# Moving the packed values to the head of the small-tile run, and four smaller moves, in a fused attention and gated feed-forward kernel

## The chip, the cores and the metric

The kernel runs on one core of a Trainium2 chip. Its time is the device time of one execution in microseconds (us): 409.43 us, the median of three runs (408.6 to 409.56). Engines are named as in the profile: PE multiplies matrices, PEld loads its weights, DVE is the vector engine, ACT the scalar engine, POOL GpSimd, SP the queue that issues DMAs.

## The reference

For each of 8 batches, 8 heads of 576 rows and 64 columns go through two attentions in a row; the result `x` (576 x 512) then goes through a gated feed-forward block:

```
p_packed = softmax(p @ k^T / 8) @ v                    # 32 packed rows a head
x        = softmax(q @ p_packed^T / 8) @ p_packed      # 576 x 64 a head
h        = relu(x @ w_in);  u, v = left and right half of h      # 512 columns each
v_n      = (v - mean(v)) / sqrt(var(v) + 1e-6)         # along the columns
v_s      = w_spatial @ v_n + b_spatial                 # along the 576 rows
out      = (u * v_s) @ w_out
```

All of it is float32, and the kernel keeps that precision by splitting numbers in a high and a low part (`_h`, `_l`) and multiplying high by high, high by low and low by high.

## The kernel before

The program works batch by batch, and the loop over `b` (line 1108) is a pipeline three batches deep, written by hand: while the feed-forward block of batch `b` runs (`ff`, `att`), the query attention of `b + 1` (`nxt`) is prepared, the packed values of `b + 2` (`far`) are made, and the packed scores of `b + 3` (`further`). PE, DVE, ACT and POOL keep the order in which the calls stand (lines 35 to 46), so each engine is a strict queue; the SP queue issues loads and stores in order too.

PSUM is cut into four tiles of two banks, `q0` to `q3`, handed round by name: a new user of a tile waits until the last reader of the old content is done. SBUF tiles come from pools under a tag; tag `o` (two buffers) holds the kept half of the last value chunk (`part`) and the four output blocks of a batch; tag `vn` (two buffers) holds the split of `T3` and `T4`; tags `v_h` and `v_l` (one buffer each) hold the split values and, later in the batch, the product parts `P1`, `P5`, `P57` and `U`.

One batch on PE has these stages: `value` (the right half of `x @ w_in`, three groups of row chunks, each summed over the two halves `r` of the heads); turns of small matrices; `up` (the left half); then a run of small matmuls, in order `query_scores` (names `qT,ppT`), `mix(1)` (`w_in_sb,ppT`: the packed rows times one half of `w_in`, so that the query weights can be applied to that product), `pack_values` (`v_sb,p1T`), `mix(0)`, `pack_scores` (`kT,pT`); then the four `gate` groups (`wsp_h,v_h` and so on); then seven `product` blocks of 12 matmuls, by which the 2 x 2 blocks of the last matrix product are made from seven products: A11, S1, A12 (summed onto A11), S4 (onto S1), S3, S2, A22 (onto S3).

Beside the gates and products, DVE and ACT make the query softmax of `nxt` in halves 0 and 1 (`query_max`, `query_sub`, `query_exp`, `query_sum`, `query_norm`, `query_turn`, `query_hi`, `query_lo`, `query_tail`), apply the gate (`gated`), and form and split the blocks (`block_sum`, `block_hi`, `block_lo`: `g21`, `g22`, `T1` to `T4`). A product that is summed onto a PSUM tile waits until that tile has been read (`keep_part` for P1 and P5, `add_part` for P57). At the end come `U = P1 + S2`, `out12 = U + S4`, `out22 = U + P57`, `out21 = U + A22`, each written to its own tile of tag `o` and stored.

Of the kernel before, what the change touches and what calls it, by code (L numbers as in the profile page):

```python
# [11 lines left out]
F32 = mybir.dt.float32  # L12
F32R = mybir.dt.float32r
AF = mybir.ActivationFunctionType
ALU = mybir.AluOpType
# [4 lines left out]
P = 128  # L20
B, H, S, D, NP = 8, 8, 576, 64, 32
DM, DF = 512, 1024
FH = DF // 2
# [26 lines left out]
def body(ctx: ExitStack, tc, q, k, v, vt, p, w_in, w_sp, b_sp, w_out, out):  # L50
# [11 lines left out]
    pe, dve, act, pool = (  # L62
        InOrder(tc, e) if x in PIN else e
        for e, x in ((nc.tensor, "t"), (nc.vector, "v"), (nc.scalar, "s"), (nc.gpsimd, "g"))
    )
# [4 lines left out]
    two = ctx.enter_context(tc.tile_pool(name="two", bufs=2))  # L70
    small = ctx.enter_context(tc.tile_pool(name="small", bufs=3))
    psum = ctx.enter_context(tc.tile_pool(name="ps", bufs=1, space=bass.MemoryType.PSUM))

    def on(i):

        return lambda: psum.tile([P, 2, 512], F32, tag=f"ps{i}", name=f"ps{i}_t")

    def by_turns(*quarters):
        turn = itertools.cycle([on(i) for i in quarters])
        return lambda: next(turn)()  # L80
# [4 lines left out]
    def mm(out_ap, lhsT, rhs, start, stop, more=False):  # L85

        pe.matmul(out_ap, lhsT=lhsT, rhs=rhs, start=start, stop=stop, skip_group_check=more)
# [27 lines left out]
    def load_v(b):  # L115
        v_sb = io.tile([P, NC + 1, H * D], F32, tag="v", name="v_sb")
        nc.sync.dma_start(v_sb[:, :NC, :], v[b])
        nc.sync.dma_start(v_sb[:TAIL, NC, :], vt[b])
        loaded["v", b] = v_sb
# [111 lines left out]
    A11, A12, A22, S1, S2, S3, S4, A21 = range(8)  # L231
# [70 lines left out]
    class Attention:  # L302
# [172 lines left out]
        def mix(self, x, psum):  # L475
# [4 lines left out]
            for r in range(2):  # L480
                for j in range(NJ):
# [5 lines left out]
                        True,  # L487
                    )

        def mix_hi(self, x, rs=slice(0, 2)):  # L490
            act.copy(self.m_h[:, x, rs, :], self.ms[x][:, rs, :])

# [4 lines left out]
    class FeedForward:  # L497
# [12 lines left out]
        def chunks(self, g):  # L510
            return [c for c in (2 * g, 2 * g + 1) if c <= NC]

        def value(self, g, psum=None, js=(0, 1), ns=(0, 1, 2)):
            a_h, a_l, m_h, m_l = (getattr(self.att, x) for x in ("a_h", "a_l", "m_h", "m_l"))
            if g not in self.ps:
                self.ps[g] = psum()
            terms = ((a_h, m_h), (a_h, m_l), (a_l, m_h))
            if g == 2:
                terms = terms[:2]
            steps = [(r, n) for r in range(2) for n in range(len(terms))]  # L520
            if self.b == 0:
                steps.sort(key=lambda rn: rn[1])
            for r, n in steps:
                if n not in ns:
                    continue
                aa, ww = terms[n]
                for i in js[: len(self.chunks(g))]:
                    c = 2 * g + i
                    mm(
                        self.ps[g][:, i, :],  # L530
                        aa[:, r, c * P : (c + 1) * P],
                        ww[:, 1, r, :],
                        (r, n) == steps[0],
                        (r, n) == steps[-1],
                    )
# [241 lines left out]
            self.put(o, 0, 1)  # L777

        def out21(self, fs=slice(0, 2)):
            if fs.start == 0:  # L780
                self.o21 = self.out_block()
            self.add_part(self.o21, "U", A22, fs)
            self.put(self.o21, 1, 0, fs)

        def out22(self):
            o = self.out_block()
            dve.tensor_tensor(o, self.part("U"), self.part("P57"), op=ALU.add)
            self.put(o, 1, 1)


# [16 lines left out]
    att, nxt, far, further = (Attention(b) for b in range(4))  # L807
    keep_warm(2, 9)
    att.pack_scores(by_turns(0, 3))
    ff = FeedForward(0, att)  # L810
# [296 lines left out]
    q0, q1, q2, q3 = 1, 2, 3, 0  # L1107
    for b in range(1, B):
        att, nxt, far = nxt, far, further
        further = Attention(b + 3) if b + 3 < B else None  # L1110
        ff = FeedForward(b, att)
        ff.value(2, psum=on(q0))
        ff.value(0, psum=on(q1))
        ff.relu(2)
        ff.value(1, psum=on(q2))
        ff.relu(0)
        ff.relu_tail()
        ff.stats(2)
        ff.inverse(2)
        ff.stats(0)  # L1120
        ff.inverse(0)
        ff.relu(1)
        if far:
            far.pack_turn(on(q3), ff.ps[2])
        if nxt:
            nxt.packed_turn(ff.ps[2])
            nxt.packed_turned()
        if far:
            far.pack_turned()
        ff.stats(1)  # L1130
        ff.inverse(1)
        ff.norm(2)
        ff.norm(0)
        ff.up(0, psum=on(q1))
        ff.up_relu(0)
        ff.norm_hi(0)
        ff.norm(1)
        ff.norm_lo(0)
        ff.up(1, psum=on(q2))
        ff.norm_hi(2)  # L1140
        ff.up_relu(1)
        ff.up(2, psum=on(q0))
        ff.up_relu(2)
        ff.tail_hi()
        ff.norm_lo(2)
        ff.up(3, psum=on(q3))
        ff.up_relu(3)
        ff.norm_hi(1)
        if nxt:
            nxt.query_scores(psum=by_turns(q1, q2))  # L1150
            nxt.query_tiles()
            if far:
                load_q(b + 2)
            nxt.mix(1, psum=on(q0))
            nxt.query_spread(0)
            nxt.query_spread(1)
            nxt.mix_hi(1)
            if far:
                far.pack_values(on(q3))
                far.packed()  # L1160
                if further:
                    load_v(b + 3)
            nxt.mix_lo(1)
        ff.norm_lo(1)
        if nxt:
            nxt.mix(0, psum=on(q1))
            nxt.mix_hi(0)
            if further:
                further.pack_scores(psum=by_turns(q2, q3))
                if b + 4 < B:  # L1170
                    load_k(b + 4)
                for r in range(2):
                    further.pack_max(r)
                    further.pack_exp(r)
            nxt.mix_lo(0)
            nxt.query_max(0)
            nxt.query_sub(0)
            nxt.query_exp(0)
            if further:
                further.pack_sum()  # L1180
        if further:
            turns = (q0, q1, q2, q3)
        else:
            turns = (q3, q2, q0, q1) if nxt else (q1, q2, q0, q3)
        if not nxt:
            for cs in ((0, 1), (2, 3)):
                ff.gate((0, 1), "hm", cs, psum=by_turns(*turns[:2]))
        for e, i in enumerate(turns):
            ff.gate((e,), "hmlt" if nxt or e > 1 else "lt", psum=on(i))
            if nxt and e == 1:  # L1190
                nxt.query_sum(0)
                nxt.query_norm(0)
            ff.gated(e)
            if nxt and e == 0:
                nxt.query_max(1)
                nxt.query_sub(1)
                nxt.query_exp(1)
            elif e == 1:
                ff.block_hi("g11")
                ff.block_sum("T1")  # L1200
                ff.block_hi("T1")
                ff.block_lo("g11")
                if nxt:
                    nxt.query_turn(0)
                    nxt.query_hi(0)
                ff.block_lo("T1")
            elif nxt and e == 2:
                nxt.query_lo(0)
                nxt.query_tail(0)
                nxt.query_sum(1)  # L1210
                nxt.query_norm(1)
        ff.product(A11, "g11", psum=on(turns[0]))
        ff.block_hi("g21")
        ff.block_sum("T3")
        ff.block_lo("g21")
        ff.keep_part("P1", A11)
        ff.block_hi("g22")
        ff.block_sum("T2")
        ff.product(S1, "T1", psum=on(turns[1]))
        ff.block_hi("T3")  # L1220
        ff.block_lo("g22")
        ff.keep_part("P5", S1)
        ff.block_lo("T3")
        ff.block_hi("T2")
        ff.product(A12, "g21", onto=A11)
        ff.out11()
        ff.block_sum("T4")
        ff.block_lo("T2")
        ff.block_hi("T4")
        ff.product(S4, "g22", onto=S1)  # L1230
        ff.block_lo("T4")
        if nxt:
            nxt.query_turn(1)
            nxt.query_hi(1)
        ff.product(S3, "T3", psum=on(turns[2]))
        ff.add_part("P57", "P5", S3)
        if nxt:
            nxt.query_lo(1)
            nxt.query_tail(1)
        ff.product(S2, "T2", psum=on(turns[3]))  # L1240
        ff.add_part("U", "P1", S2)
        ff.out12()
        ff.product(A22, "T4", onto=S3)
        if nxt:
            ff.out22()
            ff.out21()
        else:
            for f in range(2):
                ff.out21(slice(f, f + 1))
            ff.out22()  # L1250
        q0, q1, q2, q3 = turns[0], turns[1], turns[3], turns[2]


_INS = ["q", "k", "v", "vt", "p", "w_in", "w_sp", "b_sp", "w_out"]
# [51 lines left out]
```

## Time and profile before

| | us |
|---|---|
| median of the runs | 409.43 (408.6 to 409.56) |
| the profiled execution: its own time | 407.98 |
| the profiled execution: its span, first to last instruction | 406.2 |
| busy: PE, DVE, ACT, POOL | 394.9, 332.9, 192.7, 74.1 |

The profile is of one execution, and all rows below are of it. PE's matmuls overlap at their ends, so the time from one matmul's start to the next one's start is what a matmul costs; the "us" of a group runs from its first start to its last modelled end. A timeline merges equal instructions that follow each other. All helpers record through line 43, so groups are told apart by the names of their tiles.

### The profile page before, as it was taken

To read this page: it belongs to the slowest core of one execution; us is meant where nothing else is said; L and a number is where in the kernel's file an instruction comes from. 1 tells how busy PE (TensorE), PEld (TensorE's weight loads), DVE (VectorE), ACT (ScalarE), POOL (GpSimd) and SP (SyncE) were. 2 spreads that over 40 slices of the span, in tenths; PEclk is the share of its full clock that TensorE was granted. 3 is DMA by queue.
4 is the path that set the end of the run, shared out by engine and by line. 5 is a ranking of instruction groups with operands and counts; after the bars stand their busy time and mean duration, and the time that the engine had idled before them with its cause. 6 is when DMAs were issued, how large, how long until landed. Compare 5 with 4: busy or idle time off the path is not lost.

```text
span 406.2 us, 8936 instructions
## 1 busy us (share of the span) xinstructions
PE 394.9 (97%) x3800; PEld 354.5 (87%) x3800; DVE 332.9 (82%) x567; ACT 192.7 (47%) x291; POOL 74.1 (18%) x98
## 2 busy tenths in 40 slices
PE   7999999999999999999999999999999999999993
PEld 5768977799799879999699888999799889999993
DVE  2597799979799779977899788995899789978563
ACT  3587865766435353434634273244634272526140
POOL 1566445644000120002100030001200030004000
PEclk9999999999999999999999999999999999999998
DMA  7999057730810227020530205002300200020002
GB/s 306 382 383 397 20 178 305 241 116 2 293 66 31 87 81 278 2 85 34 224 129 31 87 13 225 0 29 89 120 0 30 87 2 2 0 102 17 2 30 88
DMA packets 16620, 46.62 MB, mean 115 GB/s; under 512 B 1346, under 2 KB 10562, under 8 KB 13764
## 3 DMA queue, kind: packets, MB, share of 16 engines
q1 hardware_dynamic: 16580, 46.05, 31.1%
q8 instruction: 30, 0.49, 0.5%
q14 instruction: 10, 0.08, 0.1%
HBM read 36.61 MB, written 9.44 MB: 113 GB/s over the span
## 4 chain that ended last, share of the span: by engine, by line
PE 94%; DVE 3%; POOL 1%; issue 1%; DMA 1%; POOLq 0%; DVEq 0%
PE ps_t L43 94%; DVE nmax L43 1%; POOL bits L43 1%; DMA out_t<-o 1%; DVE bits L43 0%; DVE t L43 0%; DVE o L43 0%; DVE sm_t L43 0%; DVE w_in_sb L43 0%; DVE pp L43 0%; DVE mx L43 0%; DVE prod L43 0%; POOL ident masks.py:199 0%; DVE rtot L43 0%; POOL ident masks.py:197 0%
## 5 line engine op out<-in xcount | busy, mean ns | idle before, releaser
L43 PE MATMUL ps_t<-wsp_h,v_h 128*128 128x288 f32 x256 | 55.9, 300 | 0.0
L43 PE MATMUL ps_t<-wsp_l,v_h 128*128 128x288 f32 x256 | 54.5, 295 | 0.0
L43 POOL TENSOR_TENSOR rstd<-mv,eps 128x2 f32<-128x2 f32 (+2 forms) x26 | 6.9, 265 | 245.5 <-DVE mv L43 245.4
L43 PE MATMUL ps_t<-t,wout_h 128*128 128x288 f32 x232 | 48.3, 294 | 0.0
L43 PEld LDWEIGHTS ps_t<-wsp_h,v_h 128*128 128x128 f32 x256 | 40.8, 188 | 3.8 <-DVE m_l L43 1.9
L43 PEld LDWEIGHTS ps_t<-wsp_l,v_h 128*128 128x128 f32 x256 | 41.5, 189 | 0.0
L43 ACT CAST g_h<-u 128x576 fp32r<-128x576 f32 x24 | 16.1, 674 | 49.4 <-DVE u L43 49.1
L43 PE MATMUL ps_t<-wsp_h,v_l 128*128 128x288 f32 x256 | 39.4, 296 | 0.0
L43 PEld LDWEIGHTS ps_t<-t,wout_h 128*128 128x128 f32 x232 | 38.0, 188 | 0.0
L43 PEld LDWEIGHTS ps_t<-wsp_h,v_l 128*128 128x128 f32 x256 | 35.9, 189 | 0.5 <-issue 0.5
L43 PE MATMUL ps_t<-t,wout_l 128*128 128x288 f32 x116 | 32.3, 294 | 0.0
L43 PE MATMUL ps_t<-g_h,wout_h 128*128 128x288 f32 x104 | 30.1, 305 | 0.6 <-DVE pp L43 0.6
L43 PE MATMUL ps_t<-g_h,wout_l 128*128 128x288 f32 x104 | 29.1, 295 | 0.0
L43 PE MATMUL ps_t<-a_h,m_h 128*128 128x288 f32 x128 | 28.1, 301 | 0.0
L43 PE MATMUL ps_t<-a_h,m_l 128*128 128x288 f32 x128 | 27.4, 296 | 0.0
L43 PE MATMUL ps_t<-a_l,m_h 128*128 128x288 f32 x128 | 27.4, 296 | 0.0
L43 DVE TENSOR_TENSOR u<-ps_t,u 128x576 f32<-128x576 f32 x28 | 21.0, 749 | 7.3 <-PE ps_t L43 7.3
L43 PE MATMUL ps_t<-m_l,a_h 128*128 128x512 f32 x80 | 25.8, 390 | 0.0
L43 PE MATMUL ps_t<-m_h,a_h 128*128 128x512 f32 x80 | 25.8, 391 | 0.0
L43 ACT ACTIVATE sm_t<-sm_t 128x576 f32<-128x576 f32 x16 | 11.0, 685 | 27.5 <-DVE sm_t L43 23.7
L43 DVE TENSOR_TENSOR o<-ps_t,prod 128x576 f32<-128x576 f32 (+1 forms) x15 | 10.7, 717 | 15.4 <-DMA out_t<-o 15.1
L43 ACT COPY part<-ps_t 64x512 f32<-64x512 f32 x8 | 4.7, 583 | 39.2 <-DVE o L43 39.2
(136 smaller groups left out, 989.6 us busy)
## 6 DMA issues: line engine op xcount, KB each, us to landing
out_t<-o SPq DMA_DIRECT2D x31, 288.0 KB, 2.3
v_sb<-in_v SPq DMA_DIRECT2D x8, 1024.0 KB, 8.1
qT<-in_q SPq DMA_DIRECT2D x7, 1152.0 KB, 5.4
kT<-in_k SPq DMA_DIRECT2D x7, 1152.0 KB, 8.4
raw<-in_w_in SPq DMA_DIRECT2D x4, 1024.0 KB, 12.7
raw<-in_w_out SPq DMA_DIRECT2D x2, 1024.0 KB, 9.8
kT<-in_k SPq DMA_DIRECT2D x2, 576.0 KB
qT<-in_q SPq DMA_DIRECT2D x2, 576.0 KB, 12.8
```

The costliest lines, as they stand in the source:

```text
L43: return lambda *a, **k: self.tc.keep_in_program_order(call(*a, **k))
```

## The change

`pack_values` and `packed` move from between the two mixes to the head of the small-tile run. Both mixes follow each other, and each is copied whole out of PSUM by ACT (`mix_keep`, into tag `vn`); its high part is then cast from that copy, its low part formed from it. The PSUM tiles are handed out in another order. `query_sum(1)` and `query_norm(1)` move from the third gate into the products, the splits of the blocks are reordered, and the value groups 2 and 0 are made by halves of the heads, so that half 1 of the query weights is needed later. `out21` and `out22` are formed in place, in `U` and in `P57`; in the last batch `out22` comes ahead of `out21`.

```diff
+        def mix_keep(self, x):
+            kept = two.tile([P, 2, FH], F32, tag="vn", name="kept")
+            act.copy(kept, self.ms[x])
+            self.ms[x] = kept
...
-        def value(self, g, psum=None, js=(0, 1), ns=(0, 1, 2)):
+        def value(self, g, psum=None, js=(0, 1), ns=(0, 1, 2), rs=(0, 1)):
...
-                if n not in ns:
+                if n not in ns or r not in rs:
...
-            if fs.start == 0:
-                self.o21 = self.out_block()
-            self.add_part(self.o21, "U", A22, fs)
-            self.put(self.o21, 1, 0, fs)
+            o = self.part("U")
+            self.add_part(o, "U", A22, fs)
+            self.put(o, 1, 0, fs)
...
-            o = self.out_block()
-            dve.tensor_tensor(o, self.part("U"), self.part("P57"), op=ALU.add)
+            o = self.part("P57")
+            dve.tensor_tensor(o, self.part("U"), o, op=ALU.add)
...
-        ff.value(2, psum=on(q0))
-        ff.value(0, psum=on(q1))
+        for r in range(2):
+            ff.value(2, psum=on(q0), rs=(r,))
+            ff.value(0, psum=on(q1), rs=(r,))
...
+        if far:
+            far.pack_values(on(q1))
+            far.packed()
+            if further:
+                load_v(b + 3)
         if nxt:
-            nxt.query_scores(psum=by_turns(q1, q2))
+            s0, s1, m1, m0 = (q2, q0, q3, q1) if far else (q1, q2, q0, q3)
+            nxt.query_scores(psum=by_turns(s0, s1))
             nxt.query_tiles()
             if far:
                 load_q(b + 2)
-            nxt.mix(1, psum=on(q0))
             nxt.query_spread(0)
+            nxt.mix(1, psum=on(m1))
+            nxt.mix_keep(1)
             nxt.query_spread(1)
+            nxt.mix(0, psum=on(m0))
+            nxt.mix_keep(0)
             nxt.mix_hi(1)
...
-            turns = (q0, q1, q2, q3)
+            turns = (q3, q1, q2, q0)
         else:
-            turns = (q3, q2, q0, q1) if nxt else (q1, q2, q0, q3)
+            turns = (q2, q0, q3, q1) if far else (q1, q2, q0, q3)
...
-                nxt.query_sum(1)
-                nxt.query_norm(1)
...
+        if nxt:
+            nxt.query_sum(1)
+        ff.keep_part("P5", S1)
...
+            ff.out22()
             for f in range(2):
                 ff.out21(slice(f, f + 1))
-            ff.out22()
-        q0, q1, q2, q3 = turns[0], turns[1], turns[3], turns[2]
+        q0, q1, q2, q3 = turns[0], turns[3], turns[1], turns[2]
```

On PE, the end of `up` and the small-tile run of a batch with all four stages (`v_sb` the packed values, `qT` the query scores, `w_in_sb` the mixes, `kT` the packed scores, `wsp_h` the first gate). Before:

```order
L43 MATMUL ps_t<-a_h,m_l 128x288 x2
L43 MATMUL ps_t<-qT,ppT 32x288 x16
L43 MATMUL ps_t<-w_in_sb,ppT 32x512 x8
L43 MATMUL ps_t<-v_sb,p1T 32x64 x40
L43 MATMUL ps_t<-w_in_sb,ppT 32x512 x8
L43 MATMUL ps_t<-kT,pT 32x288 x16
```

The same place on PE in the change:

```order
L43 MATMUL ps_t<-a_h,m_l 128x288 x2
L43 MATMUL ps_t<-v_sb,p1T 32x64 x40
L43 MATMUL ps_t<-qT,ppT 32x288 x16
L43 MATMUL ps_t<-w_in_sb,ppT 32x512 x16
L43 MATMUL ps_t<-kT,pT 32x288 x16
L43 MATMUL ps_t<-wsp_h,v_h 128x288 x2
```

The packed values stand ahead of the query scores, and the two mixes are one piece of 16.

On DVE, from the fourth `gated` (`u<-ps_t,u`) to the end of the products of the same batch (`sm` the query sum, `at` the query turn, `prod<-ps_t,prod` first P57 and then U). Before, with the two rows of the query sum that lead up to it:

```order
L43 RECIPROCAL sm<-sm 128x18
L43 TENSOR_TENSOR sm_t<-sm_t,sm 128x576
L43 TENSOR_TENSOR u<-ps_t,u 128x576
L43 TENSOR_TENSOR u<-u 128x2x288
...
L43 TENSOR_TENSOR t<-u,t 128x576
L43 TENSOR_TENSOR g<-u,g 128x576
L43 TENSOR_TENSOR t<-g,t 128x576 x2
L43 STREAM_TRANSPOSE at<-sm_t 128x576
L43 TENSOR_TENSOR prod<-ps_t,prod 128x576
L43 TENSOR_TENSOR a_l<-at,a_h 128x576
L43 CAST a_h<-a_l 128x64
L43 TENSOR_TENSOR prod<-ps_t,prod 128x576
```

The same place on DVE in the change:

```order
L43 TENSOR_TENSOR t<-u,t 128x576
L43 TENSOR_REDUCE sm<-sm_t 128x18
L43 TENSOR_SCALAR sm<-sm 128x18
L43 RECIPROCAL sm<-sm 128x18
L43 TENSOR_TENSOR t<-g,t 128x576
L43 TENSOR_TENSOR sm_t<-sm_t,sm 128x576
L43 TENSOR_TENSOR g<-u,g 128x576
L43 STREAM_TRANSPOSE at<-sm_t 128x576
L43 TENSOR_TENSOR prod<-ps_t,prod 128x576
L43 TENSOR_TENSOR t<-g,t 128x576
L43 TENSOR_TENSOR a_l<-at,a_h 128x576
L43 CAST a_h<-a_l 128x64
```

The sum and the norm of half 1 stand behind the fourth `gated` and ahead of P57; the low part of T4 (the last `t<-g,t`) stands behind P57.

On DVE, the end of the last batch. Before:

```order
L43 TENSOR_TENSOR t<-g,t 128x576 x2
L43 TENSOR_TENSOR prod<-ps_t,prod 128x576 x2
L43 TENSOR_TENSOR o<-ps_t,prod 128x576
L43 TENSOR_TENSOR o<-ps_t,prod 128x288 x2
L43 TENSOR_TENSOR o<-prod 128x576
```

In the change:

```order
L43 TENSOR_TENSOR t<-g,t 128x576
L43 TENSOR_TENSOR prod<-ps_t,prod 128x576
L43 TENSOR_TENSOR o<-ps_t,prod 128x576
L43 TENSOR_TENSOR prod<-prod 128x576
L43 TENSOR_TENSOR prod<-ps_t,prod 128x288 x2
```

`out22` stands ahead of the two halves of `out21`, and both are written into the product parts instead of a tile of tag `o`.

## Rows read from the trace of the kernel before

**Rows 1.** The page: PE's busy time, and the chain that ended last.

```profile
PE 394.9 (97%) x3800; PEld 354.5 (87%) x3800; DVE 332.9 (82%) x567; ACT 192.7 (47%) x291; POOL 74.1 (18%) x98
...
PE 94%; DVE 3%; POOL 1%; issue 1%; DMA 1%; POOLq 0%; DVEq 0%
```

**Rows 2.** PE timeline of batch 2's small-tile run: start us, us, what.

```profile
147.12 0.42 PE L43 MATMUL ps_t<-a_h,m_l 128*128 128x288 f32 x2
147.47 1.23 PE L43 MATMUL ps_t<-qT,ppT 64*32 64x288 f32 x32
148.46 1.27 PE L43 MATMUL ps_t<-w_in_sb,ppT 64*32 64x512 f32 x16
149.66 1.68 PE L43 MATMUL ps_t<-v_sb,p1T 128*32 128x64 f32 x76
151.13 0.63 PE L43 MATMUL ps_t<-w_in_sb,ppT 64*32 64x512 f32 x4
...
152.07 1.38 PE L43 MATMUL ps_t<-kT,pT 64*32 64x288 f32 x32
```

**Rows 3.** PE timeline of batch 6's run, which has no packed values.

```profile
332.45 2.18 PE L43 MATMUL ps_t<-w_in_sb,ppT 64*32 64x512 f32 x32
334.56 0.53 PE L43 MATMUL ps_t<-wsp_h,v_h 128*128 128x288 f32 x2
```

**Rows 4.** PE timeline of batch 3's run.

```profile
193.81 1.83 PE L43 MATMUL ps_t<-qT,ppT 64*32 64x288 f32 x28
...
196.67 1.68 PE L43 MATMUL ps_t<-v_sb,p1T 128*32 128x64 f32 x76
```

**Rows 5.** PE timeline of batch 5's run.

```profile
287.12 1.72 PE L43 MATMUL ps_t<-qT,ppT 64*32 64x288 f32 x28
...
289.88 1.68 PE L43 MATMUL ps_t<-v_sb,p1T 128*32 128x64 f32 x76
```

**Rows 6.** DVE timeline, 184 to 279: the last output block of batches 2 and 4.

```profile
184.71 0.76 DVE L43 TENSOR_TENSOR o<-ps_t,prod 128x576 f32<-128x576 f32 x1 [4.10 <-DMA out_t<-o]
...
277.92 0.76 DVE L43 TENSOR_TENSOR o<-ps_t,prod 128x576 f32<-128x576 f32 x1 [4.00 <-DMA out_t<-o]
```

**Rows 7.** DVE timeline of the end of the last batch.

```profile
399.09 1.61 DVE L43 TENSOR_TENSOR o<-ps_t,prod 128x576 f32<-128x576 f32 x3
402.23 0.76 DVE L43 TENSOR_TENSOR o<-prod 128x576 f32<-128x576 f32 x1 [1.53 <-DMA out_t<-o]
```

**Rows 8.** PE timeline of batch 1's products, around the start of A12.

```profile
124.98 0.43 PE L43 MATMUL ps_t<-t,wout_h 128*128 128x288 f32 x2
125.32 0.40 PE L43 MATMUL ps_t<-g_h,wout_h 128*128 128x288 f32 x1
125.56 0.30 PE L43 MATMUL ps_t<-g_h,wout_l 128*128 128x288 f32 x1
```

**Rows 9.** ACT timeline of the same stretch: the cast of g21, the copy of P1.

```profile
124.06 0.67 ACT L43 CAST g_h<-u 128x576 fp32r<-128x576 f32 x1 [4.10 <-DVE u L43]
124.64 0.63 ACT L43 COPY prod<-ps_t 128x576 f32<-128x576 f32 x1
```

**Rows 10.** DVE timeline of batch 1, 121 to 132: query sum, fourth gated, P57, low part.

```profile
121.31 0.75 DVE L43 TENSOR_REDUCE sm<-sm_t 128x18 f32<-128x576 f32 x1
...
123.28 0.75 DVE L43 TENSOR_TENSOR u<-ps_t,u 128x576 f32<-128x576 f32 x1
...
130.48 0.76 DVE L43 TENSOR_TENSOR prod<-ps_t,prod 128x576 f32<-128x576 f32 x1
131.15 0.75 DVE L43 TENSOR_TENSOR a_l<-at,a_h 128x576 fp32r<-128x576 f32 x1
```

**Rows 11.** PE timeline of batch 1: first product's start, and the value group behind the last.

```profile
122.08 0.29 PE L43 MATMUL ps_t<-g_h,wout_h 128*128 128x288 f32 x1
...
133.43 0.39 PE L43 MATMUL ps_t<-m_h,a_h 128*128 128x512 f32 x1
```

**Rows 12.** ACT timeline of batch 1's run: a pass over a whole mix.

```profile
103.44 1.01 ACT L43 CAST m_h<-ps_t 128x1024 fp32r<-128x1024 f32 x1 [0.61 <-PE ps_t L43]
```

More of the change, by code (lines that the diff above doesn't have):

```diff
@@ L1153, in body @@
                 load_q(b + 2)
-            nxt.mix(1, psum=on(q0))
             nxt.query_spread(0)
+            nxt.mix(1, psum=on(m1))
+            nxt.mix_keep(1)
             nxt.query_spread(1)
+            nxt.mix(0, psum=on(m0))
+            nxt.mix_keep(0)
             nxt.mix_hi(1)
[L1158 to L1163, printed above, removed]
         ff.norm_lo(1)
         if nxt:
-            nxt.mix(0, psum=on(q1))
-            nxt.mix_hi(0)
             if further:
-                further.pack_scores(psum=by_turns(q2, q3))
+                further.pack_scores(psum=by_turns(s0, s1))
                 if b + 4 < B:
@@ L1174, in body @@
                     further.pack_exp(r)
-            nxt.mix_lo(0)
+            nxt.mix_lo(1)
+            nxt.mix_hi(0)
             nxt.query_max(0)
@@ L1178, in body @@
             nxt.query_exp(0)
+            nxt.mix_lo(0)
             if further:
@@ L1214, in body @@
         ff.block_sum("T3")
+        ff.block_hi("T3")
         ff.block_lo("g21")
         ff.keep_part("P1", A11)
+        ff.block_sum("T2")
         ff.block_hi("g22")
-        ff.block_sum("T2")
         ff.product(S1, "T1", psum=on(turns[1]))
-        ff.block_hi("T3")
         ff.block_lo("g22")
-        ff.keep_part("P5", S1)
         ff.block_lo("T3")
         ff.block_hi("T2")
+        if nxt:
+            nxt.query_sum(1)
+        ff.keep_part("P5", S1)
         ff.product(A12, "g21", onto=A11)
         ff.out11()
+        ff.block_lo("T2")
+        if nxt:
+            nxt.query_norm(1)
         ff.block_sum("T4")
-        ff.block_lo("T2")
         ff.block_hi("T4")
         ff.product(S4, "g22", onto=S1)
-        ff.block_lo("T4")
         if nxt:
@@ L1236, in body @@
         ff.add_part("P57", "P5", S3)
+        ff.block_lo("T4")
         if nxt:
```

## The prediction, made before the change was timed

> **What bounds the kernel now.** First the page: PE is busy 394.9 of a span of 406.2 us, and 94% of the chain that ended last is PE's [rows 1]. So PE is idle for some 11 us, in the first batch, which the change leaves as it is, and at the end of the program. Nothing can be won by making DVE or ACT faster as such; a gain must come from a matmul that starts sooner after the one before it, or from that end. I therefore read PE's timeline by starts, and looked for places where the next start is later than that of equal matmuls elsewhere (0.13 us apart for 288 columns, 0.23 for 512). There are four kinds.
>
> First, the run of small tiles. The query scores, in tiles of 64x32, start at 147.47; the mix follows 0.99 later, the packed values, in tiles of 128x32, 1.20 later, the second mix 1.47 later, and the packed scores, again in 64x32, 0.94 after that [rows 2]. The same mix costs 1.20 where the tile shape changes behind it and 0.94 where it stays. Batch 6 has no packed values, and its two mixes with a change of shape behind take 334.56 - 332.45 = 2.11 [rows 3]: 0.91 for the first if the second takes 1.20.
>
> Second, late landings. In batches 3 and 5 the scores and first mix take 196.67 - 193.81 = 2.86 and 289.88 - 287.12 = 2.76 [rows 4, 5], against 149.66 - 147.47 = 2.19 in batch 2 [rows 2]. The cause stands a stage earlier on DVE: the last output block of the batch before waits 4.10 and 4.00 us for a store that has to leave its buffer of tag `o` [rows 6]. Behind that block, in the queues of DVE and ACT, stand `part`, the statistics and the splits of the next batch, up to the relus that free the PSUM tiles for the query scores.
>
> Third, the end. DVE does U, out12 and out21 from 399.09 on, then out22 idles for the same kind of landing and starts at 402.23 [rows 7].
>
> Fourth, the products. A12's first matmul is due at 125.24 (two starts behind 124.98), starts at 125.32, and the next comes 0.24 later instead of 0.13 [rows 8]: 0.08 of wait and 0.10 of restart. It waited for the copy of P1, which ran 124.64 to 125.27 behind the cast of g21 on ACT [rows 9], and that cast waited for the fourth `gated`, held on DVE by the query sum and norm of half 1, 121.31 to 123.28 [rows 10]. S4 shows the 0.10 again. Batches 1, 2, 3, 4 and 6 have this, some 0.28 each.
>
> **The change part by part.** The order of the small tiles: with the packed values ahead of the scores, the first mix has the second behind it, in its own shape, and takes 0.91 instead of 1.20. The change of shape from `up` to the first small tile stands as before, the packed values end in tiles of 64x32 and have the scores behind them where they had the second mix. So 0.29 a batch goes, in the five batches (1 to 5) that have the stage: **1.43 us**. No row shows `up` followed by the packed values. The nearest is `up` followed by the scores, two starts at 0.13 and then 0.35 from the first to 147.47, so 0.09 lost [rows 2]; I take that, which changes nothing. Bounds: a change of shape costs at least that 0.09 of drain and at most the 0.29, so the term lies between 0.45 and 1.43. The Trainium skill says that a change of tiling mode, not of tile, drains TensorE (TensorEngine Tiling (Array Packing), Key Properties). By the rule alone every switch is only such a drain, and at 0.09 each the sum would be 1.0 us smaller; the row prices this one at 0.29, because half of the tiles run behind the others when the mix ends.
>
> The mixes copied whole: two copies and two casts of ACT a batch where two casts were; a pass is 1.01 us [rows 12], so 2.0 us of ACT are added beside the gates, where ACT is idle for whole microseconds (4.10 before one cast [rows 9]). They free the PSUM tiles of gates 0 and 1 sooner than the low parts did. Priced at nothing. If the cover fails, the first gate waits for a copy that ends about 1 us behind its mix, while the second mix and the packed scores (0.94 + 1.31) run.
>
> The output blocks in place: no block waits for a landing any more, so the two late runs fall back to 2.19: 0.67 + 0.57 = **1.24 us**. The other batches lose DVE's ordinary wait there too (1.53 in the last one [rows 7]), which cost PE nothing.
>
> The end: out22 comes before out21 and has no landing to wait for. DVE's queue is U, out12 at 399.09, out22, then the halves of out21, which wait for no landing and whose product was done in time for them before: without out22 they and out12 end at 399.09 + 1.61 = 400.70, and with one more block at 0.67 [rows 10] at 401.4. Before, the last block ends at 402.23 + 0.76 = 402.99. The last store goes **1.55 us** earlier; it is issued behind three others, and half as big. Bounds: 1.2 if the stores queue, 1.7 if the smaller one lands sooner.
>
> The products: here the change adds waits. Behind the fourth `gated` DVE now has the splits, the query sum and norm, T4, the turn and only then P57, for which A22 waits. I add it up from the start of that `gated`, about 0.22 behind A11's: 0.78 to the cast of g21 (123.28 to 124.06 [rows 9, 10]) and as much again until T3 is formed, 0.58 and 0.55 on ACT for the cast of T3 and the copy of P1, 0.70 for the cast of g22 [rows 9]: 3.4 when its low part starts on DVE. From there five blocks, the turn counted as one, at 0.67 (130.48 to 131.15 [rows 10]), and the sum and norm, 1.97 [rows 10]: P57 starts at 8.7 and ends at 9.4, that is 9.6 behind A11. Seven products take 133.43 - 122.08 = 11.35 [rows 11] less 0.28 of waits, 1.58 each; A22 is due 9.48 behind A11. It waits some 0.15, and 0.10 for the restart. Next on DVE come the low part of T4 (0.67), the low query weights (0.78), their tail (0.1, taken) and U (0.76), ending 11.9 behind A11. The value group 0 now takes the tile that U reads (it took that of out12), and is due at 9.48 + 0.25 + 1.58 + 0.45 = 11.76: 0.15 more. The wait for P1 goes: its copy now ends 0.22 + 0.78 + 0.78 + 0.58 + 0.63 = 3.0 behind A11, and A12 is due at 3.16. S4's restart stays, 0.10. Old waits 0.28, new ones 0.4 to 0.45: **0.15 us** lost in each of five batches, and 0.4 in batch 5, which had none: 1.15 us. Bounds: no wait at all, a gain of 1.4, to waits of 0.8 a batch, a loss of 3.4. The value order by halves is priced at nothing: the same 28 matmuls; it moves the need for half 1 back by six matmuls, and DVE is that much later with it.
>
> **Sum**: -1.43 - 1.24 - 1.55 + 1.15 = -3.1 us. The profiled execution's time is 407.98, which gives 404.9. The median shown is 409.43, 1.45 above it; no row says why. If more late landings make up that excess, at 0.6 each, the change takes them too; if not, it gives 406.3. I forecast 405.9.
>
> **Rivals.** The products lose nothing: DVE and ACT run 0.3 sooner than added up, the waits for P57 and U vanish and the old ones too. For it: the new waits are differences of 0.15 between sums of ten durations. Against it: U ends that chain with no gap in DVE's queue. 405.9 - 1.15 - 1.4 = 403.4.
>
> The change of shape costs only a drain, and moves to another border: 1.0 less is won, 406.9. For it: 0.09 behind `up` [rows 2]. Against it: 0.91 beside 1.20 [rows 3].
>
> DVE becomes the bound: the chain from the fourth `gated` to U is 0.3 longer a batch than added up, because ACT's casts stand between its links. Six batches: 407.7. For it: every link waits for another engine.
>
> Slower than before: the same chain, with its end at value group 0, which cannot start before U has read its tile. Each 0.1 us of the chain costs 0.1 in six batches. It decides from 0.7 a batch on, when the low mix parts, now behind the packed maxima, hold the third and fourth `gated` so that the gate's end no longer starts the chain; with 0.9 a batch 5.4 us are lost against 3.1 won beside the forecast's waits: 411.3. Against it: DVE gets back its idle time before the last block (1.53 to 4.10 [rows 6, 7]), and what moves behind the gate is 1.97.
>
> The change does little beyond its end: the late landings do not occur in the timed runs and the drain is cheap, 408.5.
>
> **Chances.** The forecast 0.55 (its own range 404.4 to 407.2), no loss in the products 0.14, cheap drain 0.11, DVE the bound 0.11, little beyond the end 0.05, slower 0.04. A measurement of this kernel can tell about 0.3%, 1.2 us, from no change: faster means under 408.2, slower over 410.7. Of DVE the bound a fifth lies above 408.2, so faster 0.55 + 0.14 + 0.11 + 0.09 = 0.89, rounded to 0.88; same 0.08; slower 0.04. The range 403.4 to 408.2 leaves out 1 to 2 in 10.
>
> **What the profile after would show.** Right: two mixes as one piece of 1.85 with the packed scores behind, the small-tile run 0.29 shorter, batches 3 and 5 with no longer runs than the others; no DVE wait for a landing of an output block; the last DVE block at an end near 401.4; small waits of A22 for P57 and of a value group for U. Wrong: a piece of the run that takes longer by what the mix lost, a first gate that waits for a copy, or waits in the products over 0.6 a batch.

## The result, and the profile after

The change makes the kernel faster: 404.88 us, the median of 4 runs (404.78 to 405.54), against 409.34 of before in the same comparison (4 runs, 408.6 to 409.56). The ratio is 0.9898, with a 95% interval of 0.9881 to 0.9915. The forecast was 405.9 with a range of 403.4 to 408.2. The profiled execution took 404.85, its span is 403.1: 3.1 less than before.

The page of the kernel after, PE's busy time and the chain that ended last, beside [rows 1]:

```profile
PE 392.6 (97%) x3800; PEld 356.9 (89%) x3800; DVE 332.2 (82%) x567; ACT 204.4 (51%) x303; POOL 74.1 (18%) x98
...
PE 93%; DVE 3%; DMA 1%; ACT 1%; issue 1%; POOL 1%; SPq 0%; DVEq 0%; POOLq 0%; ACTq 0%
```

PE still sets the time. ACT's 11.7 us more are the copies of the mixes, and nothing waits for them. For the rest I add up PE's timeline by stages, from one stage's first start to the next one's, over batches 1 to 7 (small tiles: 1 to 6); "end" runs from the last matmul's start to the end of the span (406.21 and 403.06 to two places). The differences are taken before rounding.

| us | small tiles | gates | products | value | end |
|---|---|---|---|---|---|
| before | 32.68 | 105.08 | 78.79 | 44.64 | 6.66 |
| after | 29.82 | 105.09 | 79.51 | 44.99 | 5.23 |
| difference | -2.87 | +0.02 | +0.72 | +0.36 | -1.44 |

Turns and `up` are equal to 0.01. The sum is -3.2, and the first batch ended 0.08 later, which gives the 3.1 of the span. So the gain is in the small tiles and at the end, and a quarter of it is paid back in the products and the value groups.

First the start of the first gate in batches 2 and 3 of the kernel before, where the runs of [rows 2, 4] end; then PE's timeline of the kernel after, the small-tile runs of batches 2, 3 and 5 (start us, us, what):

```profile
153.38 0.53 PE L43 MATMUL ps_t<-wsp_h,v_h 128*128 128x288 f32 x2
...
200.39 0.53 PE L43 MATMUL ps_t<-wsp_h,v_h 128*128 128x288 f32 x2
```

```profile
147.24 1.73 PE L43 MATMUL ps_t<-v_sb,p1T 128*32 128x64 f32 x80
148.79 1.20 PE L43 MATMUL ps_t<-qT,ppT 64*32 64x288 f32 x32
149.76 2.13 PE L43 MATMUL ps_t<-w_in_sb,ppT 64*32 64x512 f32 x32
151.48 1.38 PE L43 MATMUL ps_t<-kT,pT 64*32 64x288 f32 x32
152.79 0.53 PE L43 MATMUL ps_t<-wsp_h,v_h 128*128 128x288 f32 x2
...
193.36 1.73 PE L43 MATMUL ps_t<-v_sb,p1T 128*32 128x64 f32 x80
...
198.90 0.53 PE L43 MATMUL ps_t<-wsp_h,v_h 128*128 128x288 f32 x2
...
288.06 2.13 PE L43 MATMUL ps_t<-w_in_sb,ppT 64*32 64x512 f32 x32
290.11 0.53 PE L43 MATMUL ps_t<-wsp_h,v_h 128*128 128x288 f32 x2
```

Read it by starts. From the packed values to the first gate it is 152.79 - 147.24 = 5.55 in batch 2 and 198.90 - 193.36 = 5.54 in batch 3; before it was 153.38 - 147.47 = 5.91 and, in batch 3, 200.39 - 193.81 = 6.58. Both mixes take 151.48 - 149.76 = 1.72 with the packed scores behind them, in their own shape; in batch 5, which has no packed scores, the same 32 matmuls take 290.11 - 288.06 = 2.05 with the gate's full tiles behind. Add start and us of a group and compare with the next start: where the shape changes, the next group starts only 0.07 to 0.08 before the group ahead ends (290.11 against 288.06 + 2.13; before, 149.66 against 148.46 + 1.27), where it stays, 0.41 before (151.48 against 149.76 + 2.13). So the price of a change is what the last matmuls ahead have still to run. (The ends are modelled, the starts are not.)

DVE's U of the last batch in the kernel before; then DVE's timeline of the kernel after at the end of batch 2 and of the last batch, beside [rows 6, 7]; then the SP queue's last issues:

```profile
398.30 0.76 DVE L43 TENSOR_TENSOR prod<-ps_t,prod 128x576 f32<-128x576 f32 x1 [0.82 <-PE ps_t L43]
```

```profile
180.28 0.75 DVE L43 TENSOR_TENSOR prod<-prod 128x576 f32<-128x576 f32 x1
181.13 0.76 DVE L43 TENSOR_TENSOR prod<-ps_t,prod 128x576 f32<-128x576 f32 x1
...
396.59 0.76 DVE L43 TENSOR_TENSOR prod<-ps_t,prod 128x576 f32<-128x576 f32 x1
...
398.06 0.75 DVE L43 TENSOR_TENSOR prod<-prod 128x576 f32<-128x576 f32 x1
398.91 0.82 DVE L43 TENSOR_TENSOR prod<-ps_t,prod 128x288 f32<-128x288 f32 x2
```

```profile
398.83 1.42 SPq L770 DMA_DIRECT2D out_t<-prod  x3
```

No output block has an idle time in brackets any more. From the start of U to the end of the last block it is 398.91 + 0.82 - 396.59 = 3.14 us; before it was 402.99 - 398.30 = 4.69.

The products of batch 1 in the kernel after: PE at A11, around A12 and S4 and in A22, then DVE's fourth `gated`, P57, the low part of T4 and U, beside [rows 8, 10, 11]:

```profile
121.73 0.29 PE L43 MATMUL ps_t<-g_h,wout_h 128*128 128x288 f32 x1
...
124.63 0.43 PE L43 MATMUL ps_t<-t,wout_h 128*128 128x288 f32 x2
124.90 0.34 PE L43 MATMUL ps_t<-g_h,wout_h 128*128 128x288 f32 x1
125.07 0.29 PE L43 MATMUL ps_t<-g_h,wout_l 128*128 128x288 f32 x1
...
126.55 0.38 PE L43 MATMUL ps_t<-g_h,wout_h 128*128 128x288 f32 x1
126.75 0.30 PE L43 MATMUL ps_t<-g_h,wout_l 128*128 128x288 f32 x1
...
132.00 0.64 PE L43 MATMUL ps_t<-t,wout_h 128*128 128x288 f32 x3
132.47 0.29 PE L43 MATMUL ps_t<-t,wout_l 128*128 128x288 f32 x1
```

```profile
121.93 0.76 DVE L43 TENSOR_TENSOR u<-ps_t,u 128x576 f32<-128x576 f32 x1 [0.39 <-PE ps_t L43]
...
130.54 0.72 DVE L43 TENSOR_TENSOR prod<-ps_t,prod 128x576 f32<-128x576 f32 x1
131.18 0.73 DVE L43 TENSOR_TENSOR t<-g,t 128x576 fp32r<-128x576 f32 x1
...
132.73 0.75 DVE L43 TENSOR_TENSOR prod<-ps_t,prod 128x576 f32<-128x576 f32 x1
```

A12 starts on time (124.90, two starts behind 124.63), and loses 0.04 to its restart; S4 loses 0.07; in A22 three matmuls take 0.47 instead of 0.40. The first of these three, at 132.00, is A22's fifth matmul, the first to use the low part of T4, which ends on DVE at 131.18 + 0.73 = 131.91; the change put it behind P57. This costs 0.06 to 0.08 in each of batches 1 to 6. In batches 3 to 6 A22's first matmul is late too, by 0.10 to 0.13 with its restart: the wait for P57. In batches 1 and 2 it is not; there the 34 starts between S4 and A22 take 4.57 instead of 4.48, a few nanoseconds each, and no row says why. The fourth `gated` now starts 0.20 behind A11 instead of 1.20, and DVE waits for PE there. P57 starts 130.54 - 121.73 = 8.81 behind A11.

### The profile page after: what moved, and what is told of

Read it like the earlier page. It is cut to its first block, busy times and chain, and to the rows that moved or that the text cites. A ratio compares the mean times of both kernels' runs of the same rounds, so it can differ in the third digit from the quotient of the medians.

```text
span 403.1 us, 8924 instructions
## 1 busy us (share of the span) xinstructions
PE 392.6 (97%) x3800; PEld 356.9 (89%) x3800; DVE 332.2 (82%) x567; ACT 204.4 (51%) x303; POOL 74.1 (18%) x98
## 4 chain that ended last, share of the span: by engine, by line
PE 93%; DVE 3%; DMA 1%; ACT 1%; issue 1%; POOL 1%; SPq 0%; DVEq 0%; POOLq 0%; ACTq 0%
PE ps_t L43 93%; DMA kT<-in_k 1%; DVE nmax L43 1%; POOL bits L43 1%; DVE prod L43 0%; ACT p L43 0%; DVE t L43 0%; DVE sm_t L43 0%; DVE w_in_sb L43 0%; ACT raw L43 0%; DVE pp L43 0%; DVE mx L43 0%; DVE o L43 0%; SPq L112 0%; SPq L108 0%
## 5 line engine op out<-in xcount | busy, mean ns | idle before, releaser
L43 PE MATMUL ps_t<-t,wout_h 128*128 128x288 f32 x232 | 49.4, 298 | 0.0
L43 ACT ACTIVATE vr<-ps_t 128x1024 f32<-128x1024 f32 (+1 forms) x18 | 16.7, 932 | 19.0 <-PE ps_t L43 19.0
L43 DVE BATCH_NORM_STATS2 bn<-vr 128x6 f32<-128x512 f32 x32 | 20.4, 673 | 3.8 <-ACT vr L43 3.7
```

The lines of the kernel that those rows point to most:

```text
L43: return lambda *a, **k: self.tc.keep_in_program_order(call(*a, **k))
```

## Experiments

Each kernel was compared with the kernel before on its own chip, so medians of different comparisons stand up to 0.8 us apart by their before (409.34 to 408.54). The stages are of the one profiled run.

| kernel | us, median (runs) | ratio to before, 95% | small tiles | products | value |
|---|---|---|---|---|---|
| before | 409.34 (4) | | 32.68 | 78.79 | 44.64 |
| after | 404.88 (4) | 0.9898 [0.9881, 0.9915] | 29.82 | 79.51 | 44.99 |
| before, blocks in place in all but the last batch | 407.18 (10) | 0.9968 [0.9948, 0.9987] | 31.46 | 78.84 | 44.63 |
| before, blocks in place, `out22` earlier | 405.6 (5) | 0.9932 [0.9905, 0.9958] | 31.46 | 78.73 | 44.63 |
| after, packed values between the mixes | 406.46 (8) | 0.9941 [0.9925, 0.9956] | 31.41 | 79.49 | 44.97 |
| after, scores ahead of the packed values | 405.91 (1) | | 30.62 | 79.44 | 44.95 |
| after, sum and norm at the third gate | 412.91 (4) | 1.0104 [1.0074, 1.0134] | 29.81 | 87.90 | 44.63 |
| after, value groups whole | 404.56 (4) | 0.9896 [0.9868, 0.9924] | 29.81 | 79.49 | 44.66 |
| after, query turn behind P57 | 403.5 (4) | 0.9877 [0.9857, 0.9896] | 29.81 | 78.66 | 44.74 |
| the same, copies of P1 and P5 ahead of casts | 402.27 (4) | 0.9848 [0.9827, 0.9869] | 29.82 | 77.33 | 44.61 |
| the same, query sum in the gap for ACT | 402.43 (4) | 0.9848 [0.9827, 0.9869] | 29.82 | 77.33 | 44.56 |
| after, low mix parts formed from PSUM | 421.06 (1) | | 41.76 | 79.24 | 45.00 |

**The output blocks alone.** The kernel before, with the two blocks formed in place in all batches but the last:

```diff
         def out21(self, fs=slice(0, 2)):
+            if self.b < B - 1:
+                o = self.part("U")
+                self.add_part(o, "U", A22, fs)
+                self.put(o, 1, 0, fs)
+                return
...
-            o = self.out_block()
+            o = self.part("P57") if self.b < B - 1 else self.out_block()
```

> The kernel before with one part of the change alone: out21 and out22 formed in place in batches 1 to 6, the last batch and all else as before. In the trace the stage that gives here is the small-tile run of batches 3 and 5 (2.86 and 2.76 us up to the packed values instead of 2.19). Theory L: the blocks' wait for a slow landing costs PE about 0.6 us each time, the profiled execution of before had two, and the 1.4 us by which the median of before (409.34) stands above its profiled execution (407.98) are more of them: the median here comes to 406.6 to 407.0, and every run lies close to it. Rival: the excess of the median is something else: 409.34 - 1.24 = 408.1. Both: no DVE wait for a landing in batches 1 to 6, small-tile runs of batches 3 and 5 as long as the others (5.91, and 4.7 in batch 5, which has no packed scores), end as before (6.7 us from PE's last start to the end of the span).

It took 407.18 (just above the 406.6 to 407.0 expected), 1.9 under its own before (409.05 over 17 runs, 406.99 to 409.96). PE's run of batch 3 in this kernel:

```profile
194.05 1.23 PE L43 MATMUL ps_t<-qT,ppT 64*32 64x288 f32 x32
195.04 1.27 PE L43 MATMUL ps_t<-w_in_sb,ppT 64*32 64x512 f32 x16
196.24 1.68 PE L43 MATMUL ps_t<-v_sb,p1T 128*32 128x64 f32 x76
```

The 2.86 of [rows 4] are 2.19 here, and batch 5 loses its 0.56 too: from 32.68 to 31.46, 1.23 before rounding, the forecast term, by this edit alone. The median moves by 0.6 more than that, and the spread goes: nine of these ten runs lie within 0.5 us, the 17 of before over 3.0. So the edit takes away most of the excess of the median of before over its profile. That it was late landings, of which the timed runs had more than the profiled one, is inferred; the timed runs leave no trace.

**With the end as well**: the two blocks in place in all batches, and `out22` ahead of `out21` in the last.

```diff
...
-            self.add_part(self.o21, "U", A22, fs)
-            self.put(self.o21, 1, 0, fs)
+            o = self.part("U")
+            self.add_part(o, "U", A22, fs)
+            self.put(o, 1, 0, fs)
...
-            o = self.out_block()
+            o = self.part("P57")
...
+            ff.out22()
             for f in range(2):
                 ff.out21(slice(f, f + 1))
-            ff.out22()
```

> Kernel before with the output blocks alone changed: out21 and out22 in place in all batches, and out22 ahead of out21 in the last one. Theory: the end gives its 1.40 on top of what the blocks in place give, whatever stands ahead of it: 406.99 - 1.40 = 405.6, ratio to before some 0.991, with small-tile runs as in the in-place run (5.91, and 4.71 in batch 5). Rival: part of the end's 1.40 came from the products of the last batch, which the other edits moved, and the end alone gives under 1.0: 406.0 or more.

405.6, and an end of 403.4 - 398.20 = 5.2 us from the last matmul: the edit gives the 1.4 by itself, and the rival falls. DVE's last blocks in this kernel stand as in the kernel after, with the same 0.85 between `out22` and `out21`:

```profile
398.42 0.75 DVE L43 TENSOR_TENSOR prod<-prod 128x576 f32<-128x576 f32 x1
399.27 0.82 DVE L43 TENSOR_TENSOR prod<-ps_t,prod 128x288 f32<-128x288 f32 x2
```

**The order of the small tiles.** The kernel after with the packed values back between the mixes, and with the PSUM tiles as before:

```diff
-            far.pack_values(on(q1))
-            far.packed()
...
             nxt.mix_keep(1)
+            if far:
+                far.pack_values(on(q3))
+                far.packed()
...
```

> The change with the packed values back between the two mixes, and the PSUM tiles of that run as before; the whole copies, the products and the outputs stay as in the change. Theory S: the mix pays for the change of tile shape behind it, so the run is 5.9 us again in batches 1 to 4 against 5.55, 4.7 in batch 5 against 4.58, and the median is 404.88 + 4 x 0.36 + 0.13 = 406.4. Rival: the gain came from the other PSUM tiles and the copies, by which nothing waits; the run stays at 5.55 to 5.65 and the median at 404.9 to 405.3.

406.46, and the runs are 5.91 again:

```profile
148.96 1.27 PE L43 MATMUL ps_t<-w_in_sb,ppT 64*32 64x512 f32 x16
150.16 1.68 PE L43 MATMUL ps_t<-v_sb,p1T 128*32 128x64 f32 x76
151.63 0.63 PE L43 MATMUL ps_t<-w_in_sb,ppT 64*32 64x512 f32 x4
...
152.57 1.38 PE L43 MATMUL ps_t<-kT,pT 64*32 64x288 f32 x32
```

The mixes take 1.20 + 0.94, each as before the change, with the copies still there: the order makes the 0.36, not the copies. The PSUM tiles went back together with the order, but none of these rows has an idle time in brackets, and the next kernel moves the values with the tiles of the change kept.

**Which small tiles pay.** The kernel after with the scores first, then the packed values, then both mixes:

```diff
-            far.pack_values(on(q1))
-            far.packed()
...
             nxt.query_scores(psum=by_turns(s0, s1))
             nxt.query_tiles()
...
+            far.pack_values(on(q1))
+            far.packed()
             nxt.query_spread(0)
             nxt.mix(1, psum=on(m1))
```

> Kernel after with the query scores ahead of the packed values, both mixes still one piece behind them. It tells where the price of leaving the 128x32 and 64x32 tiles lies. Theory S (any of the small kinds pays some 0.36 once, when the packed values' tile shape follows it in the middle): the run is as long as with the values between the mixes, 5.91, and the scores take some 1.3 instead of 0.97; time about 406.4. Rival (only the wide 512-column mixes pay it, since half of their tiles trail at the end): the run stays at 5.55 and the time at 404.9.

Neither: the run is 5.76.

```profile
147.82 1.23 PE L43 MATMUL ps_t<-qT,ppT 64*32 64x288 f32 x32
148.98 1.68 PE L43 MATMUL ps_t<-v_sb,p1T 128*32 128x64 f32 x76
...
152.24 1.40 PE L43 MATMUL ps_t<-kT,pT 64*32 64x288 f32 x32
153.58 0.53 PE L43 MATMUL ps_t<-wsp_h,v_h 128*128 128x288 f32 x2
```

The scores take 1.16 instead of 0.97, so a shape change behind 288 columns costs 0.19, less than behind 512 (0.34 with the same packed values behind: 1.20 against half of 1.72), and it is paid once. The packed values again start 0.07 before the scores end (148.98 against 147.82 + 1.23). Of the three places tried, the packed values stand best where full tiles, not small ones, are ahead of them.

**The sum and norm back at the third gate**, the rest of the change kept:

```diff
                 nxt.query_tail(0)
+                nxt.query_sum(1)
+                nxt.query_norm(1)
...
-            nxt.query_sum(1)
...
-            nxt.query_norm(1)
```

> The change with the query sum and norm of half 1 back at the third gate, ahead of the fourth gated. Theory P: the chain from the fourth gated decides the products, and there the casts of g21 and T3 now stand ahead of the copy of P1; gated starts about 1.5 us later, P1 ends some 4.5 us behind A11's start instead of 3.0, and A12, due at 3.16, waits 1.2 to 1.4 us; P57 and U are no later than before. Products about 12.3 us a batch against 11.4; six batches: median 404.88 + 5.4 = 410. Rival: moving the two into the products is what made A22 and the value group wait, and undoing it takes 0.25 us a batch away: 404.88 - 1.5 = 403.4.

412.91, slower than before by 1.0%: the direction is right, the size (0.9 a batch) too small. Products take 1.3 to 1.6 us more in each of batches 1 to 6. DVE and PE (A11's first matmul and A12's) in batch 1 of this kernel:

```profile
121.35 0.74 DVE L43 TENSOR_REDUCE sm<-sm_t 128x18 f32<-128x576 f32 x1
...
123.32 0.75 DVE L43 TENSOR_TENSOR u<-ps_t,u 128x576 f32<-128x576 f32 x1
```

```profile
121.62 0.29 PE L43 MATMUL ps_t<-g_h,wout_h 128*128 128x288 f32 x1
...
126.22 0.40 PE L43 MATMUL ps_t<-g_h,wout_h 128*128 128x288 f32 x1 [1.26 <-ACT prod L43]
```

The fourth `gated` starts 123.32 - 121.62 = 1.70 behind A11 instead of 0.20, and nearly all of the 1.5 comes out at A12, which starts 126.22 - 121.62 = 4.60 behind A11 instead of 3.17 and waits for the copy of P1: with the cast of T3 now ahead of that copy on ACT, the chain has no slack left. The new order of the blocks needs the move behind the gate.

**Value groups whole** (the loop over `r` dropped):

```diff
-        for r in range(2):
-            ff.value(2, psum=on(q0), rs=(r,))
-            ff.value(0, psum=on(q1), rs=(r,))
+        ff.value(2, psum=on(q0))
+        ff.value(0, psum=on(q1))
```

> The change with value groups 2 and 0 each made in one piece, as before. Theory: the split by halves is what costs the value stage 0.08 us a batch (6.44 against 6.36), since group 0 then follows 0.45 us sooner and waits for U; in one piece group 0 starts 0.9 us behind the products, U is done by then, and half 1 of the query weights (its tail copied 0.3 us ahead of the products' end) is there in time: 6.36 a batch and 404.88 - 0.5 = 404.4. Rival: half 1 is not there in time, group 2 waits for it and the value stage grows by 0.3 us or more a batch: 407.

404.56, and the value stage falls from 44.99 to 44.66: with the split, group 0 starts earlier on the tile that U has still to read. So the split costs 0.33 in the traces; the timed difference is too small to tell (the interval holds the ratio of after).

**The query turn behind P57**, and U ahead of the low weights:

```diff
-        if nxt:
-            nxt.query_turn(1)
-            nxt.query_hi(1)
         ff.product(S3, "T3", psum=on(turns[2]))
         ff.add_part("P57", "P5", S3)
         ff.block_lo("T4")
         if nxt:
-            nxt.query_lo(1)
-            nxt.query_tail(1)
+            nxt.query_turn(1)
+            nxt.query_hi(1)
         ff.product(S2, "T2", psum=on(turns[3]))
         ff.add_part("U", "P1", S2)
+        if nxt:
+            nxt.query_lo(1)
+            nxt.query_tail(1)
```

> The change with DVE's order at the end of the products altered: P57 and the low part of T4 ahead of the query turn of half 1, and U ahead of the low query weights of half 1. Theory P: A22's wait for P57 and the value group's wait for U come only from where these stand in DVE's queue; P57 starts when S3 is read (8.4 behind A11 instead of 8.8), U 0.5 sooner, and both waits go with their restarts. The products fall from 11.41 to 11.2, the value stage from 6.44 to 6.37, in six batches: median 404.88 - 1.5 = 403.4. Rival: half 1 of the query weights is 1.1 us later and the second half of value group 2 now waits for it, or the turn's cast on ACT holds something else: value stage 6.6 or more, median 405 or above.

403.5, as expected: A22 starts on time and its fifth matmul too, and U's wait shrinks to 0.03 a batch in four batches. The restarts of A12 and S4 stay: 11.15 in batches 1 and 5, and 11.34 in the other four, where the starts between S4 and A22 are again a little wider apart.

**The copies of P1 and P5 ahead of the casts of T3 and T2**, on top of that:

```diff
-        ff.block_hi("T3")
         ff.block_lo("g21")
         ff.keep_part("P1", A11)
+        ff.block_hi("T3")
...
+        ff.keep_part("P5", S1)
         ff.block_lo("T3")
         ff.block_hi("T2")
...
-        ff.keep_part("P5", S1)
```

> As the kernel with the later turn, and on ACT the copies of P1 and P5 ahead of the casts of T3 and T2. Theory P: what is left in the products are the restarts of A12 (0.05) and S4 (0.08 to 0.10), since the two copies end just before they are due; 0.5 us sooner they cost nothing. Products 11.07 to 11.1, as in batch 5 of the kernel before: median 402.6. Rival: the casts, now later, hold the low parts of T3 and g22 and with them P57: products stay at 11.2, median 403.4.

402.27, with the next kernel (the same ratio) the fastest of all: the interval of its ratio lies under that of the kernel after, and it is 1.5% under before. PE at A11 and around A12, and DVE's P57, in batch 1:

```profile
122.78 0.29 PE L43 MATMUL ps_t<-g_h,wout_h 128*128 128x288 f32 x1
...
125.68 0.43 PE L43 MATMUL ps_t<-t,wout_h 128*128 128x288 f32 x2
125.94 0.29 PE L43 MATMUL ps_t<-g_h,wout_h 128*128 128x288 f32 x1
126.07 0.29 PE L43 MATMUL ps_t<-g_h,wout_l 128*128 128x288 f32 x1
```

```profile
130.88 0.76 DVE L43 TENSOR_TENSOR prod<-ps_t,prod 128x576 f32<-128x576 f32 x1
```

The matmuls start 0.13 apart across the border, and seven products take 11.07 in each of batches 1 to 6, as only batch 5 did before. P57 starts 130.88 - 122.78 = 8.10 behind A11, 0.71 sooner than in the kernel after. These 11.07 and 6.36 of value are what the waits of the kernel after are counted from: 0.32 to 0.36 a batch in the products of batches 1 to 6, and 0.03 to 0.08 in the value groups behind them.

**The query sum in DVE's gap for ACT**, on top of that:

```diff
+        if nxt:
+            nxt.query_sum(1)
         ff.block_lo("g22")
...
-            nxt.query_sum(1)
```

> As the kernel with the copies first, and the query sum of half 1 ahead of the low part of g22, in the 0.5 us in which DVE waits for the cast of g22. Theory P: the chain behind it is 0.5 us shorter; if the copies first already leave no wait, nothing is gained: 402.6 again, else what was left of P57's or U's wait goes. Rival: the low part of g22 comes 0.6 us later and S4 waits for it: products 11.3 or more, median 404.

402.43, stage for stage the same: PE has no wait left in the products for DVE to save.

**Without the copies of the mixes** (`mix_keep` empty, so the low parts are formed from PSUM):

```diff
-            act.copy(kept, self.ms[x])
-            self.ms[x] = kept
+            del kept
```

> The change without the two whole copies: the casts and the low parts read the mixes in PSUM, in the order of the change. Theory C: the copies are what lets gate 0 start; without them its PSUM tile is read until the low part of mix 1, which stands behind the packed maxima on DVE, ends 8.4 us behind the start of the small-tile run, and gate 0, due at 5.55, waits 2.9 us in batches 1 to 4; the time is 404.85 + 11 = 416. Rival: the copies only add work to ACT and the tiles would be free anyway: 404.9.

421.06, one run. PE in batch 2 of this kernel, and below it the same time by stretches (us, then busy of PE, PEld, DVE, ACT, POOL with counts, granted clock, DMA share, GB/s):

```profile
160.38 0.50 PE L43 MATMUL ps_t<-wsp_h,v_h 128*128 128x288 f32 x2 [2.92 <-DVE m_l L43]
...
161.52 0.68 PE L43 MATMUL ps_t<-wsp_l,v_h 128*128 128x288 f32 x2
```

```profile
154.00:157.00 3.00, 3.00 (x85) 1.97 (x70) 2.39 (x3) 1.01 (x1) 0.00 (x0) 1.00 0.71 240
157.00:160.40 3.40, 0.48 (x13) 0.05 (x1) 3.20 (x7) 2.04 (x5) 0.00 (x0) 1.00 1.03 378
160.40:162.00 1.60, 1.60 (x8) 1.60 (x9) 1.57 (x3) 0.81 (x2) 0.00 (x0) 0.65 1.01 421
162.00:164.00 2.00, 2.00 (x10) 2.00 (x10) 1.06 (x3) 0.40 (x1) 0.00 (x0) 0.50 0.99 413
```

The first gate waits 2.92 us for the low part `m_l`, which on DVE now stands behind the packed maxima. It does so in batches 1 to 4, which gives 11.9 us of small tiles. The other 4.3 us nobody had priced: in batches 1 to 3 the gates take 16.4 to 16.5 instead of 15.03. In the stretches above PE is busy for 0.48 of the 3.40 us ahead of the first gate at a granted clock of 1.00, and behind it the clock is 0.50 (1.2 GHz) for some microseconds.

## Why the prediction was right, step by step

**PE bounds the kernel.** Right: adding ACT work cost nothing, and every gain and loss but that of the end is a matmul's start.

**The order of the small tiles, -1.43.** Measured -1.64, by another sum: four batches at 0.364, 0.13 in batch 5, 0.05 in batch 6. The sizes were off in both directions and in part cancelled. Both mixes took 1.72, not the 1.85 expected: with their own shape on both sides each costs 0.86. The packed values behind `up` take 1.55 where they took 1.47 (0.08 lost, priced at nothing). And batch 5 was counted in full, though it has no packed scores: there the mixes have the gate's full tiles behind, and 2.05 - 1.72 = 0.33 of shape change stays. By the Trainium skill's rule a change of mode drains TensorE (TensorEngine Tiling (Array Packing), Key Properties). The traces agree for the changes of this run: the next shape starts 0.07 before the modelled end of what is ahead. They decide against one price of 0.09 for it, since what is lost is 0.09, 0.19 or 0.33 by what stands ahead.

**The copies of the mixes, nothing.** Right: the gates take 105.08 before and 105.09 after. They are needed all the same: without them the first gate waits 2.92 us in four batches, and the time is 421.06.

**The late landings, -1.24.** Measured -1.23, and shown alone by the blocks in place.

**The end, -1.55.** Measured -1.44. The forecast's own numbers, 402.99 and 401.4, give 1.59. From the start of U to the end of the last block DVE gained 1.55 (4.69 to 3.14). The other 0.11 went in the stores: from the last block's end to the span's end it is 403.06 - 399.73 = 3.33, before 406.21 - 402.99 = 3.22. That three issues of SP now follow each other closely is a likely cause, which no run isolates; the bound of 1.2 for stores that queue allowed for it.

**The products, +1.15.** Measured +1.08. DVE's chain came out as added up: P57 was put at 8.7 behind the fourth `gated`, some 8.9 behind A11, and starts at 8.81; U was to end at 11.9 and ends at 11.75. With the value groups behind them, batches 1 to 6 wait 0.39 to 0.43 each (0.4 to 0.45 forecast). But the parts are others, and that they add up so well is in part luck. A22's wait for P57, put at 0.25 with its restart, is 0.02 in two batches and 0.10 to 0.13 in four. The low part of T4, priced at nothing behind P57, costs 0.06 to 0.08, and the restart of A12, taken as gone, 0.04. U's wait, put at 0.15, is 0.03 to 0.08, and it is the price of the value halves, which the forecast put at nothing: with the groups whole the value stage is 44.66. Batch 5, which had no wait, loses 0.39. Batch 7 loses 0.12, where the cast of T3 stands ahead of the copy of P1; with the copies first it is back at its 10.93.

**The excess of the median, 1.45.** This is the step that failed in size: I let about 1.0 of it stay, and none did. After's median equals its profiled run to 0.03. The blocks in place alone take most of the excess away, so that more late landings in the timed runs of before are its likely cause, not seen in a trace. That is why the time came out 1.0 under the forecast, on a sum of -3.1 that was right. A profiled run can stand above its median for another reason: that of the kernel with the copies first took 403.27 against 402.27, and its first batch ended at 88.06 instead of 87.07 in the kernel after.

**The rivals.** No loss in the products: it lost 1.08, and 402.27 shows that the order of the blocks, not DVE's total, decides. A cheap drain: refuted by the packed values put back. DVE as the bound, and slower than before: both wanted the chain longer than added up, and it came out 0.1 to 0.15 shorter. One kernel is slower than before, the one with the sum and norm at the third gate (412.91), but by the copy of P1 on ACT, at A12; its value stage, where that rival saw the loss, takes 44.63, as before.

## What to carry to other kernels

Put the narrow or odd tile shape at the border where a stage changes shape anyway, and leave a shape behind matmuls that have little left to run when the next could start; look at what stands beside each group, not only at what it is. A chain through two engines that ends at a reused PSUM tile has a slack that can be added up row by row; order the copies that free a tile ahead of casts that are due later. And where a kernel's timed runs spread more than its profile explains, look for a buffer that is reused before its store has landed.

## What was not expected of the hardware

- A change of tile shape has no one price: 0.09 us behind `up` (288 columns, full tiles), 0.19 behind the scores (288 columns, 64x32), 0.33 behind the mixes (512 columns, 64x32). In each case the first matmul of the next shape starts 0.07 before the modelled end of the last one ahead. Among the turns of small matrices the step from 128x128 to 128x64 tiles and back shows no such loss: the starts stay 0.11 apart.
- Around the end of an idle time of PE of 2.92 us, the granted clock fell to 0.50, with matmuls of 288 columns 0.24 apart instead of 0.13, and cost 1.4 to 1.5 us more in three of four batches; in the fourth, with the same wait, the gates took 14.99. What makes the difference stays open.
